# Retention then an expert layer: the third batch's transposes go to the crossbar, the fourth's first ones to another queue, eight stores are held back

## The chip, the cores and the metric

The kernel runs on one core of one Trainium2 chip. The metric is the device time of one execution in microseconds (us): before the change 311.78, the median of three runs (311.3 to 312.04).

## What is computed

Two stages, one after the other. The first is retention, attention without a softmax: for each of 8 batches and 8 heads, 576 positions of 64 values, the scores `q k^T / 8` are multiplied by a decay `gamma^(i - j)` for `j <= i` and by zero elsewhere, and then by `v`. The second takes the 4608 x 512 result as tokens through a layer with `g(h) = h * sigmoid(beta * h)`, 512 to 2048 and back to 512.

```python
def _attn_ref(q, k, v):
    B, H, S, D_ = q.shape
    scores = 1.0 / np.sqrt(D_) * np.matmul(q, k.transpose(0, 1, 3, 2))
    gamma = 1.0 - 2.0 ** (-5.0 - np.arange(H, dtype=np.float32))
    rel = np.arange(S)[:, None] - np.arange(S)[None, :]
    Dmat = np.where(rel >= 0, gamma[:, None, None] ** rel[None, :, :], 0.0)
    return np.matmul(scores * Dmat[None, :, :, :], v)

def _moe_ref(x, w_in, w_out, beta):
    h = x @ w_in
    return (h * (1.0 / (1.0 + np.exp(-beta * h)))) @ w_out
```

Inputs and output are float32; the kernel multiplies in bfloat16.

## The kernel before

**Tiles.** A batch's first 512 positions are 4 chunks of 128; its last 64 are joined with another batch's to a tail tile. `seq` lists all of them in order: indices 0 to 3 are batch 0's chunks, 4 to 7 batch 1's, 8 to 11 batch 2's, 12 to 15 batch 3's, 16 and 17 two tails, 18 to 21 batch 4's, and so on. The second stage works in blocks of 512 tokens, one a batch, and one block of tails.

**A batch's preparation.** `load_q` and `load_kv` bring queries, and keys and values chunk by chunk, through SyncE's DMA queue (lines 81 and 94). `pre_q` (L247) scales the queries to bfloat16, `pre` copies a chunk's keys (L273) and scales its values (L255); for batch 2 and later all of it is on GpSimd (POOL). Queries and keys have to be transposed as well. Up to batch 2 TensorE does it: `t_q` (L297, two per batch, 8 transposes of 128x128 each) and `t_k` (L303, one per chunk, 4 each) write to PSUM, and ScalarE (ACT) or VectorE (DVE) copies the result to `qT` or `kT` (L298, L304). From batch 3 on the DMA's crossbar does it: `x_q` and `x_k` issue a `dma_start_transpose` each for half a batch's queries or a pair of chunks, and `x_tail` for a tail, all through ACT's DMA queue (L281). `XB` is the first batch for which this holds.

**A batch's attention.** `first(i)` does a pair of chunks i and i + 1: the state update `a_st(i)` (L396, which needs no transposed tile, with ACT copies L401) and the scores `a_sc` of both (L323, from `kT` and `qT`; DVE masks them, L333). `outputs` multiplies the masked scores by the values (L366), adds the part of the state (L351), and copies to `xT` (L384), the second stage's input.

**The second stage.** `up` multiplies four 128-row pieces of `w_in` by `xT` (L413) and applies the activation on ACT (L415). `down` multiplies by `w_out` (L426); when the last of 2048 is added, DVE copies the result to `ot` (L433) and SyncE stores it (L436, 256 KB for a quarter of a block).

**The order is written out by hand.** `fill` is the list of all `up` and `down` calls. `merged` walks through it, and before item n it emits every other step with a due position of at most n. Each engine, and each DMA queue, runs its instructions in the order in which they were emitted; an instruction that waits for another engine or for a transfer holds up what comes behind it on its engine. Items 0 to 15 are block 0's `up`, from `d0` = 16 its `down`; from `u1` = 32 block 1's `up` (20 half items for two chunks each, then 6 whole ones), from 58 its `down`; `base[n]` is where block n starts: 74, 106, 138 for 2, 3, 4 (`base[1]` is 42). Where the steps around the change stand:

| step | due position before |
|---|---|
| `load_q(2)`, loads of chunks 8, 9 | 10.4 |
| loads of chunks 10 and 11 | 24.6, 26.1 |
| stores of block 0 | after 25, 26, 27, 31 |
| `pre_q(2, 0..3)`, on POOL | 41 to 44 |
| `pre(8)` to `pre(11)`, on POOL | 46.5 to 48 |
| `t_q(2, 0)`, `t_q(2, 1)` | 47.5, 48.5 |
| `t_k(8)`, `t_k(9)`; `first(8)` | 49.5, 50.5; 53 |
| `load_q(3)`; loads of chunks 12, 13 | 47; 49, 51 |
| `t_k(10)`, `t_k(11)`; `first(10)`; `outputs(8)` | 58.5, 59.5; 62; 67 |
| `pre_q(3, 0..3)`; `pre(12)`, `pre(13)` | 57 to 60; 61, 62 |
| `x_q(3, 0)`, `x_q(3, 1)`, `x_k(3, 0)`, on ACT's queue | 63, 64.5, 66.5 |
| stores of block 1 | after 61, 65, 69, 73 |
| loads of chunks 14, 15; `first(12)` | 64, 66; 77 |
| `load_tail(0)`, `x_k(3, 1)`, `load_tail(1)` | 78, 81.5, 88 |

Staging tiles for the output, `ot`, come from the four buffers (tag `wt`) through which the weights were loaded: blocks 0 to 3 have one each, block 4 takes block 0's again.

Of the kernel before, what the change touches and what calls it, by code (L numbers as in the profile page):

```python
# [19 lines left out]
def kernel(  # L20
# [10 lines left out]
    nc = tc.nc  # L31
# [9 lines left out]
    CB = MB // P  # L41
# [25 lines left out]

    NQ = 6
    E = CB
    XB = 3  # L70
    QB = 2
    q_tiles, kv_tiles = {}, {}

# [158 lines left out]
    batch, pair, live = {}, {}, {}  # L232
# [44 lines left out]
    def heads(t, p):  # L277
        return t[:, 2 * p:2 * p + 2, :].rearrange("p h d -> p (h d)")

    def turn(dst, src):  # L280
        nc.scalar.dma_start_transpose(dst.rearrange("p j pr s -> p (j pr) s"), src.rearrange("p j h d -> p (j h d)"))  # L281

    def x_q(b, u):
        turn(batch[b]["qT"][:, 2 * u:2 * u + 2], batch[b]["qs"][:, 2 * u:2 * u + 2])

    def x_k(b, u):
        kn, kT = pair[b, u]
        turn(kT, kn)

    def x_tail(i):  # L290
        turn(live[i]["qkT"], live[i]["qk"])
# [122 lines left out]
                             start=(ko == 0), stop=(ko == KO - 1))  # L414
        nc.scalar.activation(gts[m][:, fo, :, w], ph, ACT.Silu, scale=beta_sb[:, fo:fo + 1])  # L415

    pos_, ots = {}, {}

    def down(m, ms, f0, fn=4, n0=0, nn=d_model):

        gT = gts[m]
        if f0 == 0:
            pos_[ms] = psum.tile([P, d_model], F32, name="po", tag="mm", bufs=3)
        po = pos_[ms]
        for fo in range(f0, f0 + fn):
            nc.tensor.matmul(po[:, :nn], gT[:, fo, ms, :], w_out_sb[:, fo, n0:n0 + nn],  # L426
                             start=(fo == 0), stop=(fo == FO - 1))
        if f0 + fn < FO:
            return
        if ms == 0:  # L430
            ots[m] = stage.tile([P, MB // P, d_model], F32, name="ot", tag="wt", bufs=4)
        ot = ots[m][:, ms, n0:n0 + nn]
        nc.vector.tensor_copy(ot, po[:, :nn])  # L433
        if m < B:
            rows = out[m * S:m * S + MB].rearrange("(s i) n -> s i n", i=CB)
            nc.sync.dma_start(rows[:, ms, n0:n0 + nn], ot)  # L436
        else:
            for x in range(2):
                r0 = (2 * ms + x) * S + MB
                nc.sync.dma_start(out[r0:r0 + TL, n0:n0 + nn], ot[x * TL:(x + 1) * TL])  # L440
# [12 lines left out]
    def F(f, *a):  # L453
        return lambda: f(*a)
# [49 lines left out]
    fill = [F(up, 0, fo) for fo in range(FO)]  # L504
    d0 = len(fill)
    fill += [F(down, 0, ms, f0) for f0 in range(0, FO, 4) for ms in range(3)]
    fill += [F(down, 0, 3, f0) for f0 in range(0, FO, 4)]

    u1 = len(fill)
    fill += [F(up, 1, fo, 2 * x, 2) for x in range(2) for fo in range(10)]  # L510
    fill += [F(up, 1, fo) for fo in range(10, FO)]
    fill += [F(down, 1, ms, f0) for ms in range(MB // P) for f0 in range(0, FO, 4)]
    base = {1: u1 + 10}
    for n, m in enumerate(blocks[2:], 2):
# [6 lines left out]
    def second(i):  # L521
        for f in (a_O, lambda j: a_cross(j, False), a_x):
# [6 lines left out]
               [(d0 - 4 + 3.3 * g, F(cast_w_out, g)) for g in range(WG)],  # L529
               [(10.3, F(load_q, 1))] + [(10.3, F(load_kv, CB + n, (j,))) for n, j in keys_first],  # L530
               [(10.4, F(load_q, 2))] + [(10.4, F(load_kv, 2 * CB + n)) for n in range(2)],
               [(d0 + 8.6, F(load_kv, 2 * CB + 2)), (d0 + 10.1, F(load_kv, 2 * CB + 3))],
               [(d0 + 7, F(pre_q, 1, n)) for n in range(4)] + [(d0 + 10.6, F(t_q, 1, 0)), (d0 + 12.6, F(t_q, 1, 1))],
               [(d0 + 8, F(pre, 4, (0,))), (d0 + 8, F(pre, 5, (0,))), (d0 + 9, F(pre, 4, (1,))), (d0 + 9, F(pre, 5, (1,))),
                (d0 + 12.7, F(t_k, 4)), (d0 + 12.8, F(t_k, 5)), (d0 + 13.8, F(a_sc, 4)), (d0 + 13.81, F(a_sc, 5)),
                (d0 + 14.8, F(a_st, 4)), (d0 + 15.9, F(second, 4))],
# [16 lines left out]
    def pair_prep(i, at):  # L553
        b, c = seq[i]
        if b is None:
            return [(at - 31, F(load_tail, c)), (at - 21.5, F(pre, i)), (at - 21, F(load_tail, c + 1)),
                    (at - 13, F(pre, i + 1)), (at - 12, F(x_tail, i)), (at - 9.5, F(x_tail, i + 1))]
        n, st = full.index(i), []
        if b < XB:
            if c == 0:  # L560
                st += [(at - 12 + x, F(pre_q, b, x)) for x in range(4)]
                st += [(at - 5.5, F(t_q, b, 0)), (at - 4.5, F(t_q, b, 1))]
                st += [(at - 6.5 + x / 2, F(pre, i + x)) for x in range(CB)]
            return st + [(at - 3.5, F(t_k, i)), (at - 2.5, F(t_k, i + 1))]
        if c == 0:
            st += [(at - 30, F(load_q, b))] + [(at - 20 + x, F(pre_q, b, x)) for x in range(4)]
            st += [(at - 14 + 1.5 * x, F(x_q, b, x)) for x in range(2)]
        return st + [(at - 28, F(load_kv, n)), (at - 26, F(load_kv, n + 1)), (at - 16, F(pre, i)),
                     (at - 15, F(pre, i + 1)), (at - 10.5, F(x_k, b, c // 2))]

    todo = list(range(2 * CB, len(seq), 2))
    for n in range(1, B - 1):

        take = [i for i in todo if seq[i][0] == n + 1 or n == B - 2 or seq[i] == (None, 0) and n == CB - 1]
        todo = todo[len(take):]
        lo, hi = (base[n] + 11, base[n + 1] - 12) if n == 1 else (base[n] + 3, base[n + 1] - 8)
        at = [lo + x * (hi - lo) / (len(take) - 1) for x in range(len(take))]
        if len(take) == 2 and n > 1:
            at[1] -= 6
        for i, t in zip(take, at):  # L580
            st = pair_prep(i, t) + [(t, F(first, i))]
            if seq[i][0] is None:
                st.append((t + 5, F(second, i)))
            elif seq[i][1] == 0:
                st.append((t + 2, F(a_st, i + 1)))
            else:
                st.append((t + 5, F(outputs, i - 2)))
            streams.append(st)
# [32 lines left out]
```

## Time and profile before

| what | before |
|---|---|
| time, median of 3 runs | 311.78 us |
| time of the profiled execution | 311.92 us |
| span of the profiled execution, first to last instruction | 310.1 us |
| TensorE busy | 298.5 us |
| TensorE clock granted, mean | 0.998 |
| transposes by the crossbar, all on ACT's queue | 24 of 256 KB |
| TensorE transposes L297, L303 | 48 and 48 |
| one ACT copy of `qT`, of `kT` | 1012 ns, 586 ns |
| DMA moved | 52.79 MB |

In the profile PE is TensorE's matmul, PEld its weight load, SP SyncE, and a "q" behind an engine is its sequencer, which issues DMAs. A line of the chain or the timeline gives the start in us from the span's start, the duration, the engine, the line of the kernel, what is written and read, and how many instructions are merged in it; in brackets the idle time before it and what ended that. A line of DMA issues gives the transfer, the queue, how many, and the median time from issue to landing.

### The profile page before, as it was taken

To read this page: it belongs to the slowest core of one execution; us is meant where nothing else is said; L and a number is where in the kernel's file an instruction comes from. 1 tells how busy PE (TensorE), PEld (TensorE's weight loads), DVE (VectorE), ACT (ScalarE), POOL (GpSimd) and SP (SyncE) were. 2 spreads that over 40 slices of the span, in tenths; PEclk is the share of its full clock that TensorE was granted. 3 is DMA by queue.
4 is the path that set the end of the run, shared out by engine and by line. 5 is a ranking of instruction groups with operands and counts; after the bars stand their busy time and mean duration, and the time that the engine had idled before them with its cause. 6 is when DMAs were issued, how large, how long until landed. Compare 5 with 4: busy or idle time off the path is not lost.

```text
span 310.1 us, 5363 instructions
## 1 busy us (share of the span) xinstructions
PE 298.5 (96%) x2144; PEld 157.8 (51%) x2177; DVE 106.9 (34%) x191; ACT 143.0 (46%) x256; POOL 96.0 (31%) x131
## 2 busy tenths in 40 slices
PE   7789999999999999999999999999999999999995
PEld 5544456775544454454554545455545444444444
DVE  7554476342531342434430434043405420010012
ACT  5567626995138412560186117711673037207700
POOL 4663026846524282254308031902420000000000
PEclk9999999999999999999999999999999999999999
DMA  8999999998989999999897697968852110031011
GB/s 207 221 355 387 380 232 273 233 257 179 202 197 162 224 189 235 218 212 198 133 234 107 136 205 207 201 115 192 196 76 37 68 70 0 17 88 34 0 70 68
DMA packets 123897, 52.79 MB, mean 170 GB/s; under 512 B 105680, under 2 KB 116320, under 8 KB 123872
## 3 DMA queue, kind: packets, MB, share of 16 engines
q1 hardware_dynamic: 98496, 46.15, 61.5%
q10 hardware_dynamic: 25376, 6.30, 13.6%
q8 instruction: 17, 0.28, 0.4%
q14 instruction: 8, 0.07, 0.1%
HBM read 36.71 MB, written 9.44 MB: 149 GB/s over the span
## 4 chain that ended last, share of the span: by engine, by line
PE 85%; DMA 6%; SPq 5%; DVE 1%; issue 1%; ACT 1%; POOL 1%; POOLq 0%
PE po L426 40%; PE ph L413 35%; DMA wt<-in_moe_w_in_dram 4%; SPq L94 3%; PE O L366 3%; PE sc L323 3%; DMA qn<-in_q_dram 2%; PE O L351 2%; PE st L396 2%; SPq L178 1%; POOL qs L247 1%; PE T L297 1%; PE T L303 1%; ACT gT L415 0%; DVE xT L384 0%
## 5 line engine op out<-in xcount | busy, mean ns | idle before, releaser
L415 ACT ACTIVATE gT<-ph,beta_sb 128x512 bf16<-128x512 f32 (+1 forms) x154 | 99.2, 659 | 86.3 <-PE ph L413 83.4
L413 PE MATMUL ph<-xT,w_in_sb 128*128 128x512 bf16 (+1 forms) x600 | 129.3, 365 | 3.2 <-DVE w_in_sb L186 0.9
L426 PE MATMUL po<-w_out_sb,gT 128*128 128x512 bf16 (+2 forms) x591 | 126.7, 368 | 1.1 <-issue 0.3
L413 PEld LDWEIGHTS <-w_in_sb 128*128 128x128 bf16 x616 | 58.7, 98 | 65.0 <-DVE w_in_sb L186 2.3
L426 PEld LDWEIGHTS <-gT 128*128 128x128 bf16 x608 | 57.1, 98 | 62.5
L333 DVE TENSOR_TENSOR R<-sc,causal 128x512 bf16<-128x512 f32 x71 | 44.3, 684 | 68.9 <-PE sc L323 68.9
L433 DVE COPY ot<-po 128x512 f32<-128x512 f32 (+2 forms) x38 | 25.0, 662 | 92.1 <-PE po L426 92.0
L255 POOL TENSOR_TENSOR vn<-kvn,gv 128x512 bf16<-128x512 f32 x32 | 33.4, 1042 | 22.8 <-DMA kvn<-in_v_dram 11.5
L247 POOL TENSOR_TENSOR qs<-qn,gq 128x512 bf16<-128x512 f32 x24 | 24.3, 1042 | 33.2 <-DMA qn<-in_q_dram 33.2
L273 POOL CAST kn<-kvn 128x512 bf16<-128x512 f32 x32 | 19.6, 612 | 47.7 <-DMA kvn<-in_k_dram 47.3
L401 ACT CAST sbd<-st 64x256 bf16<-64x256 f32 x48 | 17.4, 362 | 15.0 <-PE st L396 14.3
L384 DVE CAST xT<-O 128x512 bf16<-128x512 f32 x24 | 15.8, 688 | 19.6 <-PE O L366 9.6
L384 ACT CAST xT<-O 128x512 bf16<-128x512 f32 x11 | 6.4, 586 | 32.2 <-PE O L351 25.2
L396 PE MATMUL st<-vn,kn 128*128 128x128 bf16 x128 | 12.4, 219 | 0.2 <-POOL vn L255 0.2
L396 PEld LDWEIGHTS <-kn 128*128 128x128 bf16 x128 | 9.3, 98 | 5.0 <-issue 0.2
L366 PE MATMUL O<-R,vn 128*64 128x128 bf16 x288 | 10.7, 221 | 0.0
L323 PE MATMUL sc<-qT,kT 64*128 64x128 bf16 x256 | 10.3, 217 | 0.4 <-ACT kT L304 0.2
L366 PEld LDWEIGHTS <-vn 128*64 128x64 bf16 x288 | 8.5, 110 | 4.1 <-issue 3.6
L323 PEld LDWEIGHTS <-kT 64*128 64x128 bf16 x288 | 8.1, 94 | 3.8 <-ACT kT L304 1.5
L304 ACT COPY kT<-T 128x512 bf16<-128x512 bf16 x12 | 6.9, 586 | 4.8 <-PE T L303 4.8
L208 PE MATMUL ph<-warm 128*128 128x128 f32 (+1 forms) x24 | 7.0, 429 | 1.2 <-DVE warm L119 1.2
L186 DVE CAST w_in_sb<-wt 128x256 bf16<-128x256 f32 (+1 forms) x14 | 6.0, 476 | 5.2 <-DMA wt<-in_moe_w_in_dram 5.2
(56 smaller groups left out, 90.2 us busy)
## 6 DMA issues: line engine op xcount, KB each, us to landing
qn<-in_q_dram SPq DMA_DIRECT2D x16, 512.0 KB, 5.8
kvn<-in_k_dram SPq DMA_DIRECT2D x32, 256.0 KB, 5.9
kvn<-in_v_dram SPq DMA_DIRECT2D x32, 256.0 KB, 5.6
out_dram<-ot SPq DMA_DIRECT2D x31, 256.0 KB, 2.7
wt<-in_moe_w_out_dram SPq DMA_DIRECT2D x4, 1024.0 KB, 9.5
wt<-in_moe_w_in_dram SPq DMA_DIRECT2D x4, 512.0 KB, 7.5
wt<-in_moe_w_in_dram SPq DMA_DIRECT2D x2, 1024.0 KB, 11.8
out_dram<-ot SPq DMA_DIRECT2D x9, 128.0 KB, 2.4
```

Source lines behind the costliest of these rows:

```text
L247: e.tensor_tensor(batch[b]["qs"][:, cs, hs], q_tiles[b][:, hs, cs].rearrange("p h i d -> p i h d"), gq[:, cs, hs].unsqueeze(3).to_broadcas ...
L255: nc.gpsimd.tensor_tensor(live[i]["vn"][:], kv_tiles.pop(i)[:, 1], gains(gv, c), ALU.mult)
L273: nc.gpsimd.tensor_copy(kn[:, c % 2], t[:, 0])
L323: nc.tensor.matmul(view(sc[j][:, p, :]), L["kT"][r, p, :], rhs, start=True, stop=True, skip_group_check=True)
L333: nc.vector.tensor_tensor(R[:, j], sc[j][:], causal4[:] if i == CB - 1 else m_b, ALU.mult)
L366: nc.tensor.matmul(O[j * D:(j + 1) * D, p, :], vn[:, 2 * p + j, :], R[:, j, p, :], start=p == 0 and not (early and crossed), stop=early or ...
L384: (nc.scalar.copy if on_act else nc.vector.tensor_copy)(x, O[:])
L396: nc.tensor.matmul(st[:, p, :], heads(L["kn"], p), heads(L["vn"], p), start=(c == 0 and p == 0), stop=True, skip_group_check=True)
L413: nc.tensor.matmul(ph, w_in_sb[:, ko, fo * P:(fo + 1) * P], xts[m][:, ko, :, w], start=(ko == 0), stop=(ko == KO - 1))
L415: nc.scalar.activation(gts[m][:, fo, :, w], ph, ACT.Silu, scale=beta_sb[:, fo:fo + 1])
L426: nc.tensor.matmul(po[:, :nn], gT[:, fo, ms, :], w_out_sb[:, fo, n0:n0 + nn], start=(fo == 0), stop=(fo == FO - 1))
L433: nc.vector.tensor_copy(ot, po[:, :nn])
```

## The change

Batch 2 is transposed by the crossbar instead of TensorE (`XB` from 3 to 2, so `t_q(2)` and `t_k(8..11)` are gone, and `x_q(2)`, `x_k(2)` come in). The crossbar transposes of queries for batches 2 and 3, and of their first pair of keys, are issued by SyncE; the others stay with ACT. The preparation of batch 2 is emitted earlier: `pre_q(2)` at 28.5, `x_q(2, 0)` and `x_q(2, 1)` at 28.6 and 28.7 and `x_k(2, 0)` at 29.6 (ahead of the load of chunk 11, now at 29.8), `pre(8)`, `pre(9)` at 29 and 30, `pre(10)`, `pre(11)` at 40 and 40.5, `x_k(2, 1)` at 58.5. `first(8)`, `first(10)` and `outputs(8)` move to 58, 64 and 69. The eight stores of blocks 0 and 1 are put on a list, and issued four at 69.5 and four at 82.

```diff
-    XB = 3
+    XB = 2
...
-    def turn(dst, src):
-        nc.scalar.dma_start_transpose(dst.rearrange("p j pr s -> p (j pr) s"), src.rearrange("p j h d -> p (j h d)"))
+    def turn(dst, src, on_sp=False):
+        (nc.sync if on_sp else nc.scalar).dma_start_transpose(dst.rearrange("p j pr s -> p (j pr) s"), src.rearrange("p j h d -> p (j h d)"))
 
     def x_q(b, u):
-        turn(batch[b]["qT"][:, 2 * u:2 * u + 2], batch[b]["qs"][:, 2 * u:2 * u + 2])
+        turn(batch[b]["qT"][:, 2 * u:2 * u + 2], batch[b]["qs"][:, 2 * u:2 * u + 2], b <= XB + 1)
 
     def x_k(b, u):
         kn, kT = pair[b, u]
-        turn(kT, kn)
+        turn(kT, kn, b <= XB + 1 and u == 0)
...
-    pos_, ots = {}, {}
+    pos_, ots, held = {}, {}, []
+
+    def release(n):
+        for _ in range(n):
+            nc.sync.dma_start(*held.pop(0))
...
-            nc.sync.dma_start(rows[:, ms, n0:n0 + nn], ot)
+            if m < 2:
+                held.append((rows[:, ms, n0:n0 + nn], ot))
+            else:
+                nc.sync.dma_start(rows[:, ms, n0:n0 + nn], ot)
...
-               [(d0 + 8.6, F(load_kv, 2 * CB + 2)), (d0 + 10.1, F(load_kv, 2 * CB + 3))],
-               [(d0 + 7, F(pre_q, 1, n)) for n in range(4)] + [(d0 + 10.6, F(t_q, 1, 0)), (d0 + 12.6, F(t_q, 1, 1))],
+               [(d0 + 8.6, F(load_kv, 2 * CB + 2)), (d0 + 12.6, F(x_q, XB, 0)), (d0 + 12.7, F(x_q, XB, 1)),
+                (d0 + 13.6, F(x_k, XB, 0)), (d0 + 13.8, F(load_kv, 2 * CB + 3)),
+                (base[2] - 4.5, F(release, 4)), (base[2] + 8, F(release, 4))],
+               [(d0 + 7, F(pre_q, 1, n)) for n in range(4)] + [(d0 + 12.5, F(pre_q, XB, n)) for n in range(4)] + [(d0 + 10.6, F(t_q, 1, 0)), (d0 + 12.6, F(t_q, 1, 1))],
...
-        if b < XB:
+        if b == XB:
             if c == 0:
-                st += [(at - 12 + x, F(pre_q, b, x)) for x in range(4)]
-                st += [(at - 5.5, F(t_q, b, 0)), (at - 4.5, F(t_q, b, 1))]
-                st += [(at - 6.5 + x / 2, F(pre, i + x)) for x in range(CB)]
-            return st + [(at - 3.5, F(t_k, i)), (at - 2.5, F(t_k, i + 1))]
+                return [(d0 + 13, F(pre, i + x, (0,))) for x in range(2)] + \
+                       [(d0 + 14, F(pre, i + x, (1,))) for x in range(2)]
+            return [(u1 + 8 + x / 2, F(pre, i + x)) for x in range(2)] + [(u1 + 26.5, F(x_k, b, 1))]
...
-        lo, hi = (base[n] + 11, base[n + 1] - 12) if n == 1 else (base[n] + 3, base[n + 1] - 8)
+        lo, hi = (base[n] + 16, base[n + 1] - 10) if n == 1 else (base[n] + 3, base[n + 1] - 8)
```

## The prediction

> **What bounds the kernel now.** First the page's busy line, the slices and the shares of the chain that ended last.
>
> ```profile
> PE 298.5 (96%) x2144; PEld 157.8 (51%) x2177; DVE 106.9 (34%) x191; ACT 143.0 (46%) x256; POOL 96.0 (31%) x131
> PE   7789999999999999999999999999999999999995
> DMA  8999999998989999999897697968852110031011
> PE 85%; DMA 6%; SPq 5%; DVE 1%; issue 1%; ACT 1%; POOL 1%; POOLq 0%
> ```
>
> TensorE is full from the fourth slice to the last but one, so a microsecond of TensorE work taken out shortens the span by one, and a microsecond of waiting put in lengthens it by one. The DMA engines are full too until about slice 22 (170 us): whatever is handed to them there comes late. Next I read the chain of waits from 57 to 92 us, where batch 2 is prepared.
>
> ```profile
> 62.24 0.45 PE T L297 x8
> 63.12 0.45 PE T L297 x8
> 64.00 0.22 PE T L303 x4
> 64.76 0.22 PE T L303 x4
> ...
> 71.70 0.65 PE po L426 x3
> 72.40 0.39 PE T L303 x4
> ...
> 73.65 0.22 PE T L303 x4
> ```
>
> The 32 transposes of batch 2 stand in the chain, eight in 0.45 us, and nothing idles beside them: they cost what they last. By the timeline fill item 58, the first `down` of block 1, begins at 71.54; a `down` item of four matmuls takes 0.865 us. (The 0.39 at 72.40 holds 0.17 that belongs to a matmul record missing before it.)
>
> **What is removed.** Two `t_q(2, u)` of 8 transposes and four `t_k` of 4: 32 x 0.0556 = 1.78 us of TensorE. With them go copies off the bound: on ACT one of 1.01 (L298) and four of 0.59 us (L304), on DVE one of 0.69. If nothing is late, the span falls by 1.78. Moving `first(8)` from 53 to 58, `first(10)` from 62 to 64 and `outputs(8)` from 67 to 69 changes no amount of TensorE work. ACT was busy 11.80 of the 13.0 us from 57 to 70, but there it loses 2.18 us of copies against TensorE's 1.33, so it does not become the pace.
>
> **What is added.** Four crossbar transposes of 256 KB. Their price comes from the queue rows.
>
> ```profile
> q1 hardware_dynamic: 98496, 46.15, 61.5%
> q10 hardware_dynamic: 25376, 6.30, 13.6%
> ```
>
> The 24 old transposes are all of q10: 13.6% of 310.1 over 24 is 1.76 us of all 16 engines each. On q1 a transfer of 0.262 MB costs 61.5% of 310.1 x 0.262/46.15 = 1.08 us. [...]
>
> **SyncE's queue** in the same stretch:
>
> ```profile
> 56.49 1.11 SPq L94 DMA_DIRECT2D kvn<-in_k_dram  x1
> ...
> 58.81 1.46 SPq L436 DMA_DIRECT2D out_dram<-ot  x2
> 60.36 0.42 SPq L94 DMA_DIRECT2D kvn<-in_k_dram  x1
> ...
> 61.83 2.72 SPq L436 DMA_DIRECT2D out_dram<-ot  x2
> 64.60 2.04 SPq L81 DMA_DIRECT2D qn<-in_q_dram  x2
> ```
>
> Keys and values of chunk 10, two stores of block 0, chunk 11, two stores, queries of batch 3. The stores leave (4 x 1.08 = 4.3 us of DMA), and `x_q(2,0)`, `x_q(2,1)`, `x_k(2,0)` come in after chunk 10 (3 x 1.76 = 5.3): the queries of batch 3 land some 1.0 us later. What SyncE now waits for is GpSimd's scaling of batch 2's queries:
>
> ```profile
> 55.17 4.04 POOL L247 TENSOR_TENSOR qs<-qn,gq 128x512 bf16<-128x512 f32 x4 [2.40 <-DMA qn<-in_q_dram]
> 65.45 0.61 POOL L273 CAST kn<-kvn 128x512 bf16<-128x512 f32 x1 [1.57 <-DMA kvn<-in_k_dram]
> 72.84 4.04 POOL L247 TENSOR_TENSOR qs<-qn,gq 128x512 bf16<-128x512 f32 x4 [4.37 <-DMA qn<-in_q_dram]
> ```
>
> It starts when the queries land and keeps that time: its first half is ready at 57.2, all of it at 59.2, the keys of chunks 8 and 9 two casts of 0.61 later (60.4). SyncE reaches `x_q(2,0)` at 58.7, so the waits there are under 0.5 us each; queued behind them are chunk 11 and the queries of batch 3. In order of service, from the values of chunk 10 (landed about 62.3, when GpSimd takes them up at 62.83): the three transposes land at 64.1, 65.8, 67.6, the keys of chunk 11 at 68.6, and GpSimd has cast them at 69.4 (before: 66.1). The queries of batch 3 land near 73.7 (before 72.8).
>
> **Where TensorE meets them.** `first(8)`, item 58: 71.54 less 24 transposes (1.33) and less `first(8)` (0.22 + 0.55) and the state update (0.22) that move behind it is 69.2; after `a_st(8)` the scores want `qT` and `kT` at 69.4. They have been there since 67.6: cost nothing, with 1.8 us of cover; if the transposes took 3 us each it would be a stall of 2. `first(10)`, item 64: 69.2 + 0.77 + 0.22 + six items of 0.865 + `a_st(10)` 0.22 = 75.6. Its keys come by `x_k(2,1)`, which ACT issues behind the state copies of `a_st(8)`, at about 69.6, just after chunk 11 is cast (69.4). Queued behind it on ACT are only the copies of `a_st(9)`, wanted at item 69, 5 us on. How long such a transpose takes from issue to landing I bound by its own kind, each taken from the page of its window (windows 112 to 118, 144 to 146, 162 to 163, 123 to 124):
>
> ```profile
> kT<-kn ACTq DMA_TRANSPOSE x2, 3.6
> kT<-kn ACTq DMA_TRANSPOSE x1, 6.8
> kT<-kn ACTq DMA_TRANSPOSE x1, 6.0
> kT<-kn ACTq DMA_TRANSPOSE x1, 10.1
> ```
>
> 3.6 is with little beside it; 6.8 and 6.0 beside key and value loads; 10.1 beside a whole query load. At 69.6 the queue holds the end of batch 3's queries and then keys and values, nearest to the middle rows: I take 6.5, landing at 76.1, a stall of 0.5. The ends are 3.6 (none) and 10.1 (79.7, a stall of 4.1).
>
> **Batch 3's part.** Three of its transposes leave ACT's queue for SyncE's. Before, ACT stood at them from 76.0 to 83.5 while TensorE ran on `down` items that need no ACT, so nothing is gained there now. On SyncE they wait for GpSimd: queries from 73.7 to 77.7, then two chunks of 1.55 us; `x_k(3,0)` goes out near 81.5 and lands near 86. `first(12)` wants it at 91.45 + 0.22 - 1.3 = 90.4: 4 us of cover, and the same as before if that is gone (it landed 9.7 us after 80.0 then). Behind the waiting ones on SyncE are chunks 14 and 15 and the tail loads. In the old order they stood behind stores of block 1 that waited for their copies (the last until 89.6); these are held now, so they come no later. The old kernel has no transposes on two queues, so what one costs the other has no row: at least nothing, at most a wait for the other's landing. The latter holds `x_q(3,0)` until 76.1, 1 to 2 us, inside the cover of 4, and `x_k(2,1)` until 67.6, before it is reached: I take nothing. [...]
>
> **The held stores** (8 of 1.08 us of DMA) go out from item 70 on and after 82; their buffers are wanted again by block 4. Behind them on SyncE stand the tail loads, whose transposes fall at item 97. Cover over 10 us; gone, it would be a wait of some us at item 109.
>
> **Sum.** -1.78 + 0 + 0.5 = -1.3 us on the profiled execution: span 310.1 to 308.8. It took 311.92 with 1.8 around its span; the median of the runs is 311.78, which becomes 310.5. A change below 0.2% (0.62 us) can't be told from none here.
>
> **Rivals.** (1) No stall: `x_k(2,1)` lands within 6.0 us of its issue. For it: the ACT row of 162 us and the transposes of 3.6. Against: the saturated queue. -1.78, so 310.0. (2) The stall eats the gain: landing 7.2 to 8.4 us after issue, because the queries of batch 3 are still moving at 72 to 74 or chunk 11 is cast a microsecond late (65.45 now waits on its DMA). Stall 1.2 to 2.4, time 311.2 to 312.4, middle 311.7. (3) Slower, at the same place: `x_k(2,1)` shares the engines with batch 3's queries throughout, as the row of 10.1 did; then `first(10)` stalls 4.1 and the time is 311.8 - 1.8 + 4.1 = 314.1. It decides from a landing 8.4 us after issue (a stall of 1.78 + 0.62). For it: queries 1.0 us later than before, and all DMA slices at 9. Against: most of them are served by 72. (4) The change does not do what it says, ACT pacing the half items and the removed 1.33 us coming back as idle TensorE: the time then falls only by the 0.44 of the last two `t_k`, to 311.3. ACT's greater loss of work speaks against it; I put it into (2).
>
> **How the numbers follow.** The forecast, a stall of about 0.5 (0.1 to 1.1), gets 0.37; rival 1 0.25; rivals 2 and 4 0.16; rival 3 0.22. Faster by over 0.2% is the forecast and rival 1: 0.62. The likeliest is 310.5, with a range of its own of 310.1 to 311.1. For 8 in 10 the range goes from 309.5 (no stall, and the one wait of 0.60 us that TensorE has at 165 gone in part) up to 313.0, which leaves out the far part of rival 3.
>
> **What would show it.** 32 fewer L297 and L303 matmuls; 28 transposes in all, 6 of them on SyncE; item 58 near 69.2; waits of TensorE at L323 for `kT` by DMA near 69 (none) and 75.6 (0.5). Wrong would be: a wait over 1.8 us there, a wait at `first(8)`, or a new wait of TensorE after 90 us.

## The result: 3.6% slower

| what | before | after |
|---|---|---|
| time, median | 311.82 us | 322.35 us (4 runs, 320.87 to 325.56) |
| ratio to before, 95% interval | | 1.0361 [1.031, 1.0413] |
| span of the profiled execution | 310.1 us | 323.7 us |
| TensorE busy; mean granted clock | 298.5 us; 0.998 | 299.2 us; 0.979 |
| L297 and L303 transposes | 48 and 48 | 32 and 32 |
| crossbar transposes, on SyncE's queue | 24, 0 | 28, 6 |

The prediction was 310.5 with a range up to 313.0, so it was wrong, and on the other side. First the page of the changed kernel: the busy line, three rows of slices (8.1 us each), and the shares of the chain that ended last. (Lines have moved by four: `down` is now L430; the held stores go out from L421.)

```profile
PE 299.2 (92%) x2112; PEld 156.6 (48%) x2145; DVE 106.1 (33%) x190; ACT 140.1 (43%) x251; POOL 96.5 (30%) x131
PE   7799999993299989999999999999999999999995
PEclk9999999998579999999999999999999999999999
DMA  8999999999995996999869396989883110032011
PE 66%; DMA 15%; SPq 12%; POOL 4%; issue 2%; DVE 1%; POOLq 0%; ACTq 0%
```

There is one hole in TensorE's row, in slices 10 and 11 (73 to 89 us), and the granted clock drops right under it and one slice beyond. 32 matmuls are gone, yet TensorE's busy time has grown: some of the rest ran slower. TensorE's share of the chain fell from 85% to 66%; transfers went from 6% to 15%, and SyncE's queue from 5% to 12%. The next view is the timeline of TensorE there (start, duration, engine, line, written and read tiles, count; in brackets the idle time before it and what ended it).

```profile
69.01 0.39 PE L396 MATMUL st<-vn,kn 128*128 128x128 bf16 x4
69.33 0.62 PE L323 MATMUL sc<-qT,kT 64*128 64x128 bf16 x16
...
71.84 3.62 PE L430 MATMUL po<-w_out_sb,gT 128*128 128x512 bf16 x16
86.86 0.58 PE L396 MATMUL st<-vn,kn 128*128 128x128 bf16 x4 [11.40 <-ACT sbd L401]
87.71 1.03 PE L323 MATMUL sc<-qT,kT 64*128 64x128 bf16 x16 [0.27 <-DMA kT<-kn]
88.68 4.02 PE L430 MATMUL po<-w_out_sb,gT 128*128 128x512 bf16 x9
92.92 2.34 PE L430 MATMUL po<-w_out_sb,gT 128*128 128x512 bf16 x10 [0.22 <-issue]
...
119.67 0.62 PE L323 MATMUL sc<-qT,kT 64*128 64x128 bf16 x16 [1.21 <-DMA kT<-kn]
```

Up to item 64 everything is as worked out: `first(8)` begins at 69.01 (69.2 was expected), its scores wait for nothing. Then `a_st(10)`, ready to run at about 75.5, stands for 11.40 us, and not for a transpose but for ACT's state copies of `a_st(9)`. ACT's timeline says why they came so late (ACTq is its sequencer, which issues the transposes):

```profile
69.80 0.74 ACT L401 CAST sbd<-st 64x256 bf16<-64x256 f32 x2
84.53 1.33 ACTq L281 DMA_TRANSPOSE kT<-kn  x1
85.96 0.76 ACT L401 CAST sbd<-st 64x256 bf16<-64x256 f32 x2 [15.42 <-issue]
```

ACT runs nothing for 15.42 us. "issue" is time in which the profile shows no wait. What stands at its head is the one transpose that ACT issues here, `x_k(2, 1)`: reached at 70.5, gone out at 84.53. Its keys had landed at 69.18, and GpSimd had cast them to bfloat16 by 69.84:

```profile
69.23 0.61 POOL L273 CAST kn<-kvn 128x512 bf16<-128x512 f32 x1 [4.87 <-DMA kvn<-in_k_dram]
```

SyncE's queue has what did end at that moment; below it stand the same transfer and the one that followed it, in the chain that ended last:

```profile
79.53 2.40 SPq L281 DMA_TRANSPOSE qT<-qs  x1
```

```profile
79.53 4.83 DMA qT<-qs
...
84.53 3.14 DMA kT<-kn
```

This is `x_q(3, 1)`. It took 4.83 us from issue to landing: it landed at 84.35, and 0.18 us later `x_k(2, 1)` went out. Nothing in the kernel's source connects the two. The waits that the finished program carries do (DMAHW0 to DMAHW7 are the eight semaphores that this program's transfers count up when they have landed; first ACT's `x_k(2, 1)`, then SyncE's `x_q(3, 0)` and `x_q(3, 1)`, each of which waits for the earlier transfer on its own semaphore):

```
89 L281 DmaTransposeAnt kT_864<-kn_863 128x8x128 [waits DMAHW2_49,DMAHW5_49,DMAHW1_49,DMAHW7_49,DMAHW0_49,Pool_49]
...
48 L281 DmaTransposeAnt qT_1016<-qs_1015 128x8x128 [waits DVE_49,PE_49,DMAHW2_49,Activation_49,Pool_49]
51 L281 DmaTransposeAnt qT_1016<-qs_1015 128x8x128 [waits DMAHW5_49,Pool_49]
```

Semaphores 7, 0 and 1 belong to batch 2's three transposes on SyncE (0 also to a load of chunk 13's keys, landed at 78.03), 2 and 5 to batch 3's two. So `x_k(2, 1)` waits for the landing of transposes that are emitted four and a half and six items after it; the second of them landed 0.18 us before it went out. The software layer that turned the emitted calls into this program recorded them in an order of its own across the queues, and put into `x_k(2, 1)` a wait for each of the five transposes of the other queue that are recorded ahead of it.

The last view is that of the stretches around the hole (stretch, length, busy time and count of PE, PEld, DVE, ACT and POOL, granted clock, DMA share, GB/s).

```profile
75.30:79.30 4.00, 0.16 (x1) 0.00 (x0) 0.00 (x0) 0.00 (x0) 4.00 (x5) 1.00 0.96 192
79.30:86.90 7.60, 0.04 (x1) 0.07 (x2) 0.00 (x0) 0.73 (x2) 3.27 (x5) 0.50 1.17 205
86.90:92.90 6.00, 5.53 (x29) 2.55 (x31) 3.07 (x5) 0.73 (x2) 0.00 (x0) 0.50 0.74 196
92.90:100.00 7.10, 7.03 (x71) 4.08 (x72) 2.77 (x5) 1.32 (x3) 4.25 (x6) 1.00 0.87 224
```

At 79.3, after 3.8 us of idling (from 75.5), the granted clock falls from 1.00 to 0.50, and it stays so for 6.0 us after the wait is over: nine `down` matmuls take 4.02 us from 88.68, and ten take 2.34 us from 92.92. TensorE worked for 5.53 of the 6.0 us at half the clock, and half of that, an estimated 2.8 us, was lost. The sum: 11.40 + 0.27 (the scores behind it) + 1.21 (a wait for `kT` at 118) + 2.8, less 1.78 for the transposes and 0.60 for a wait that the kernel before had and this one has not, is 13.3; the spans differ by 13.6. That wait is this line of TensorE's timeline before:

```profile
165.24 2.10 PE L413 MATMUL ph<-xT,w_in_sb 128*128 128x512 bf16 x9 [0.60 <-ACT gT L415]
```

### The profile page after: what moved, and what is told of

It is laid out like the page before. It is cut to its first block, busy times and chain, and to the rows that moved or that the text cites. A ratio compares the mean times of both kernels' runs of the same rounds, so it can differ in the third digit from the quotient of the medians.

```text
span 323.7 us, 5302 instructions
## 1 busy us (share of the span) xinstructions
PE 299.2 (92%) x2112; PEld 156.6 (48%) x2145; DVE 106.1 (33%) x190; ACT 140.1 (43%) x251; POOL 96.5 (30%) x131
## 4 chain that ended last, share of the span: by engine, by line
PE 66%; DMA 15%; SPq 12%; POOL 4%; issue 2%; DVE 1%; POOLq 0%; ACTq 0%
PE po L430 33%; PE ph L413 26%; SPq L94 8%; DMA kT<-kn 4%; DMA qn<-in_q_dram 4%; DMA wt<-in_moe_w_in_dram 4%; POOL qs L247 2%; PE O L366 2%; PE sc L323 2%; SPq L81 2%; DMA qT<-qs 1%; PE O L351 1%; DMA tln<-in_k_dram 1%; PE st L396 1%; SPq L178 1%
## 5 line engine op out<-in xcount | busy, mean ns | idle before, releaser
L430 PE MATMUL po<-w_out_sb,gT 128*128 128x512 bf16 (+2 forms) x591 | 128.4, 371 | 1.2 <-issue 0.5
L430 PEld LDWEIGHTS <-gT 128*128 128x128 bf16 x608 | 57.6, 99 | 64.3 <-issue 2.9
L437 DVE COPY ot<-po 128x512 f32<-128x512 f32 (+2 forms) x38 | 25.0, 661 | 86.0 <-PE po L430 85.9
L401 ACT CAST sbd<-st 64x256 bf16<-64x256 f32 x48 | 17.4, 363 | 29.6 <-issue 15.4
L396 PE MATMUL st<-vn,kn 128*128 128x128 bf16 x128 | 12.6, 222 | 11.7 <-ACT sbd L401 11.4
L396 PEld LDWEIGHTS <-kn 128*128 128x128 bf16 x128 | 9.3, 99 | 16.6 <-issue 12.0
L323 PE MATMUL sc<-qT,kT 64*128 64x128 bf16 x256 | 10.7, 223 | 1.9 <-DMA kT<-kn 1.5
L323 PEld LDWEIGHTS <-kT 64*128 64x128 bf16 x288 | 8.4, 96 | 5.5 <-DMA kT<-kn 1.9
L262 POOL TENSOR_TENSOR kn<-tln,gq 128x512 bf16<-128x512 f32 x4 | 4.2, 1042 | 13.4 <-DMA tln<-in_q_dram 10.0
```

The source lines that it names most:

```text
L323: nc.tensor.matmul(view(sc[j][:, p, :]), L["kT"][r, p, :], rhs, start=True, stop=True, skip_group_check=True)
L396: nc.tensor.matmul(st[:, p, :], heads(L["kn"], p), heads(L["vn"], p), start=(c == 0 and p == 0), stop=True, skip_group_check=True)
```

## Experiments

Diffs are against the changed kernel, where nothing else is said. Two causes were to be told apart at first: transposes of two queues being kept apart, and the held stores or busy engines making the transfers late.

**Batch 3's transposes back to ACT**, so that SyncE has only batch 2's.

```diff
-        turn(batch[b]["qT"]..., batch[b]["qs"]..., b <= XB + 1)
+        turn(batch[b]["qT"]..., batch[b]["qs"]..., b <= XB)
...
-        turn(kT, kn, b <= XB + 1 and u == 0)
+        turn(kT, kn, b <= XB and u == 0)
```

> Batch 3's three first transposes go back to ACT's queue; batch 2's stay as in the change. Theory (cross-queue wait): in the changed kernel x_k(2,1) on ACT was issued at 84.53, just after SyncE's x_q(3,1) landed at 84.35, and the state copies behind it held TensorE for 11.4 us; here no SyncE transpose of batch 3 exists, so x_k(2,1) goes out near 70 and the time is 310.0 to 311.5. Rival (the transpose is late because the DMA engines are full): the same transfers are in the way, so the wait stays near 10 us and the time near 320.

Measured 318.83 us, ratio 1.0231 [1.0206, 1.0256]: a miss for the theory, and nearer to the rival's time. The waits shrank to 4.33 and 2.70 us but were not gone. TensorE's, ACT's and SyncE's timelines:

```profile
79.39 0.38 PE L396 MATMUL st<-vn,kn 128*128 128x128 bf16 x4 [4.33 <-ACT sbd L401]
82.47 1.03 PE L323 MATMUL sc<-qT,kT 64*128 64x128 bf16 x16 [2.70 <-DMA kT<-kn]
```

```profile
77.04 1.35 ACTq L281 DMA_TRANSPOSE kT<-kn  x1
```

```profile
71.81 1.06 SPq L94 DMA_DIRECT2D kvn<-in_v_dram  x1
```

With no later transpose on SyncE, `x_k(2, 1)` still went out at 77.04 and not at 70. The load in the last line is the values of chunk 13; it took 5.1 us and landed at 76.89, just before. The program's wait list for `x_k(2, 1)` now has only batch 2's semaphores, 7, 0 and 1, and 1 was counted up once more by that load. (The profile puts ACT's idle time down to GpSimd, which ended an instruction at the same time; from GpSimd the wait list has only the cast of chunk 11's keys, done at 68.6.) So there is a second tie: in these programs all transfers of both queues take the eight semaphores in turn, and a transfer waits for the landing of the one eight places before it in the recorded order, whatever that one carries (here from 76.89 to 77.04, 0.15 us after it).

**`x_k(2, 1)` on SyncE's queue too.**

```diff
-        turn(kT, kn, b <= XB + 1 and u == 0)
+        turn(kT, kn, b <= XB + 1 and u == 0 or b == XB)
```

> All of the change, but x_k(2,1) is issued by SyncE too, so that no ACT transpose stands between SyncE's. Theory: ACT is never held; x_k(2,1) goes out behind chunk 13 on SyncE at about 75.5 and lands near 79.5, TensorE waits some 4 us at the scores of chunk 10 instead of 11.4, time 312.5 to 315. Rival (full DMA engines): landing and wait about as in the change, near 320.

Measured 315.2 us (312.71 to 316.22), ratio 1.0101 [1.0054, 1.0149], just above the range. Of batches 2 and 3, ACT now issues only `x_k(3, 1)`, late; `x_k(2, 1)` goes out at 74.01, behind the loads on its queue, and lands at 78.76.

```profile
78.81 1.04 PE L323 MATMUL sc<-qT,kT 64*128 64x128 bf16 x16 [3.13 <-DMA kT<-kn]
```

TensorE waits 3.13 us. In the profiled execution the clock was halved from 77.9 to 84.7, which cost an estimated 2.95 us more (half of the 5.89 us that TensorE was busy in it). The spread of 3.5 us goes with the clock: the four runs, from the fastest, had a mean of 1.0, 0.995, 0.989 and 0.987.

**The stores not held.**

```diff
-            if m < 2:
-                held.append((rows[:, ms, n0:n0 + nn], ot))
-            else:
-                nc.sync.dma_start(rows[:, ms, n0:n0 + nn], ot)
+            nc.sync.dma_start(rows[:, ms, n0:n0 + nn], ot)
...
-                (base[2] - 4.5, F(release, 4)), (base[2] + 8, F(release, 4))],
```

> All of the change but the held stores: blocks 0 and 1 are stored at once again. Theory: the wait of x_k(2,1) for batch 3's queries on SyncE stays, and SyncE comes later for four stores: 321 to 326. Rival (the release of the stores in front of the tail loads, or their burst, causes the loss): 310 to 312.

Measured 314.5 us, ratio 1.0085 [1.0063, 1.0106]: 7.9 us less than the changed kernel, a miss for the theory of that moment, and above the rival's 310 to 312. On ACT and on TensorE:

```profile
71.62 1.33 ACTq L281 DMA_TRANSPOSE kT<-kn  x1
```

```profile
78.98 1.03 PE L323 MATMUL sc<-qT,kT 64*128 64x128 bf16 x16 [3.42 <-DMA kT<-kn]
```

Batch 3's transposes are on SyncE's queue as in the changed kernel, but `x_k(2, 1)` no longer waits for them. The program's wait list has batch 2's semaphores and one more: it is recorded right behind the loads of chunk 13 here, ahead of batch 3's transposes, and its own semaphore is that of the transfer eight places before it, chunk 11's values (landed 71.52, gone out at 71.62). In the changed kernel's program, with the stores out of the way, six more of SyncE's transfers are recorded ahead of it.

**The held stores alone**, in the kernel before (diff against it: `held`, `release` and the two release steps as in the change).

> The kernel before with the eight stores held and nothing else changed. Theory: SyncE is not late for anything there, 311.2 to 312.4. Rival (the held stores cost by themselves): over 314.

Measured 312.1 us over 10 runs, ratio 1.0014 [0.9996, 1.0033]. Holding cost nothing that can be measured here, where all transposes by the crossbar are on ACT's queue.

**Chunk 11 loaded early again**, at its old 26.1, to see if the keys' readiness plays a part.

```diff
-               [(d0 + 8.6, F(load_kv, 2 * CB + 2)), (d0 + 12.6, F(x_q, XB, 0)), (d0 + 12.7, F(x_q, XB, 1)),
-                (d0 + 13.6, F(x_k, XB, 0)), (d0 + 13.8, F(load_kv, 2 * CB + 3)),
+               [(d0 + 8.6, F(load_kv, 2 * CB + 2)), (d0 + 10.1, F(load_kv, 2 * CB + 3)), (d0 + 12.6, F(x_q, XB, 0)), (d0 + 12.7, F(x_q, XB, 1)),
+                (d0 + 13.6, F(x_k, XB, 0)),
```

> The change with one thing moved: the load of chunk 11 stands at its old position 26.1, ahead of SyncE's transposes, so that the keys of chunk 11 are cast near 65 instead of 69. Theory (x_k(2,1) waits for the landing of SyncE's x_q(3,1)): nothing is gained, x_k(2,1) goes out near 84 and the time stays at 319 to 326. Rival (the data of x_k(2,1) is late): it goes out near 70, time 310 to 312.

Measured 322.23 us (2 runs), ratio 1.0328 [1.0298, 1.0359]. On GpSimd and on ACT:

```profile
64.13 0.61 POOL L273 CAST kn<-kvn 128x512 bf16<-128x512 f32 x1 [0.41 <-DMA kvn<-in_k_dram]
```

```profile
83.02 1.33 ACTq L281 DMA_TRANSPOSE kT<-kn  x1
```

The keys are cast 18 us before the transpose goes out; it goes out 0.10 us after `x_q(3, 1)` landed (82.92). The wait is for the other queue's transposes and not for the keys.

**Batch 3's on ACT and the stores not held**, the first and the third edit together.

> As e1 (batch 3's transposes on ACT's queue), and the stores of blocks 0 and 1 not held. Theory (the program lets eight transfers be in flight over both queues together, each waiting for the landing of the eighth before it in recorded order; holding the stores lets SyncE's loads of chunks 14 and 15 be recorded ahead of x_k(2,1)): here x_k(2,1) follows the values of chunk 11, near 71.5, not 77.0 as in e1; TensorE waits about 3 to 4 us instead of 7.0; time 313 to 315. Rival (e1's wait was the full DMA engines): a wait of 7 us or more, 318 or above.

Measured 314.18 us, ratio 1.0081 [1.0055, 1.0107], as expected. `x_k(2, 1)` goes out at 71.71, after chunk 11's values (landed 71.62), and TensorE waits 2.91 us:

```profile
78.46 1.03 PE L323 MATMUL sc<-qT,kT 64*128 64x128 bf16 x16 [2.91 <-DMA kT<-kn]
```

Between the first experiment and this one only the hold differs, and it moves the transpose from 77.04 to 71.71: the hold makes the recorded order late, by the one tie or by the other.

**Everything for batch 2 early, on SyncE:** chunk 11 at 26.1 as in the fifth experiment, `x_k(2, 1)` at 41 on SyncE's queue.

```diff
-        turn(kT, kn, b <= XB + 1 and u == 0)
+        turn(kT, kn, b <= XB + 1 and u == 0 or b == XB)
...
-            return [...] + [(u1 + 26.5, F(x_k, b, 1))]
+            return [...] + [(u1 + 9, F(x_k, b, 1))]
```

> The change with the load of chunk 11 at 26.1 and x_k(2,1) on SyncE at 41, right behind x_k(2,0), so that every SyncE transpose comes ahead of every ACT one and x_k(2,1) is ahead of batch 3's loads. Theory: it lands near 70, before the scores of chunk 10 ask for it at 75.6; no wait of TensorE over 0.5 us between 60 and 95, no half clock, time 309.5 to 310.8, under the kernel before. Rival (the crossbar transposes cost TensorE time wherever they stand, because batch 3's loads come later for them): a wait at the scores of chunk 8 or 12, 312 or above.

Measured 313.97 us over 12 runs, ratio 1.0058 [1.0039, 1.0077]; a miss. `x_k(2, 1)` lands at 70.25 and TensorE has no wait from 60 to 95, so the rival's wait at the scores is not there either. But `x_k(3, 1)` is still on ACT's queue, beside batch 3's other three on SyncE's. ACT and TensorE:

```profile
97.53 1.80 ACTq L281 DMA_TRANSPOSE kT<-kn  x1
```

```profile
100.12 2.10 PE L413 MATMUL ph<-xT,w_in_sb 128*128 128x512 bf16 x9 [2.33 <-ACT gT L415]
```

It goes out 0.17 us after a store of SyncE's landed (97.36; issued 93.38), and behind it stood an activation of block 2's `up`, for which TensorE waited 2.33 us. The store stands eight places before it in the recorded order: the tie of the first experiment, one batch later.

**The same with all four of batch 3's on ACT.**

```diff
-..., b <= XB + 1)
+..., b <= XB)
...
-        turn(kT, kn, b <= XB + 1 and u == 0)
+        turn(kT, kn, b <= XB)
```

(and the two early steps as above)

> As e7, but batch 3's three first transposes on ACT's queue as in the kernel before. Theory: their waits fall where ACT has only copies to do, nothing on TensorE, 309.5 to 311.3. Rival (ACT held by them delays the state copies): a wait of TensorE at a state update of batch 2, 312 or above.

Measured 317.32 us over 5 runs, ratio 1.0184 [1.0156, 1.0211]. A miss, and much as the rival had it:

```profile
85.23 1.33 ACTq L281 DMA_TRANSPOSE qT<-qs  x1
```

```profile
87.47 0.61 PE L351 MATMUL O<-qT,sbd 128*128 128x128 bf16 x4 [4.67 <-ACT sbd L401]
```

`x_q(3, 0)` stands on ACT until 85.23, when the transfer eight places before it, the values of chunk 15, has landed (85.14), and state copies behind it; TensorE waits 4.67 us at L351, and the clock is halved from 85.9 to 92.7.

**All of batches 2 and 3 on SyncE**, ACT's first crossbar transposes being the tails'.

```diff
-        turn(kT, kn, b <= XB + 1 and u == 0)
+        turn(kT, kn, b <= XB + 1)
```

(and the two early steps as above)

> As e7, and x_k(3,1) on SyncE too, so that ACT issues no crossbar transpose before the tails'. Theory: in e7 x_k(3,1) stood on ACT until 97.53, when the store recorded eight transfers before it had landed (97.36), and TensorE waited 2.3 us for the activations behind it; that wait goes, the one of 1.1 us near 127 stays, and the time falls by 2.3 to 311.2 to 312.0. Rival (ACT was held by its DMA issue as such): the wait moves to another place, 313 to 314.5.

Measured 309.73 us over 12 runs, ratio 0.9943 [0.9923, 0.9963]: better than expected, and faster than the kernel before. TensorE's waits are 0.20 us at `first(8)` and 1.07 near 125, where ACT stands at the transpose of batch 4's first keys until 124.9; the clock is not halved (1.00 from 60 to 300). ACT and TensorE:

```profile
121.48 3.43 ACTq L281 DMA_TRANSPOSE kT<-kn  x1
```

```profile
125.70 1.89 PE L413 MATMUL ph<-xT,w_in_sb 128*128 128x512 bf16 x8 [1.07 <-ACT gT L415]
```

-1.78 - 0.60 + 0.20 + 1.07 = -1.1, and the span went from 310.1 to 308.9. This last wait is not the tie: what the transpose waits for by its list was done by 116.4 (GpSimd's cast at 115.4, and a store eight places before it that landed at 116.35). Its issue itself took 3.43 us, where the one before it on ACT (119.75) took 1.25; why is not shown.

**The same, batch 4's first `x_k` 2.5 items later** (diff against the version before).

```diff
-                     (at - 15, F(pre, i + 1)), (at - 10.5, F(x_k, b, c // 2))]
+                     (at - 15, F(pre, i + 1)), (at - (8 if b == XB + 2 and c == 0 else 10.5), F(x_k, b, c // 2))]
```

> As e9, and batch 4's first x_k is issued 2.5 items later on ACT, so that GpSimd's cast is done when ACT comes to it (in e7 it stood there from 124.0 to 127.4 and TensorE waited 1.1 us). Theory: that wait goes or shrinks below 0.5 us, time 310.2 to 311.2, 0.2% or more under the kernel before. Rival (the transpose then lands too late for the scores of chunk 18): a wait at the scores near 135, 312 or above.

Measured 309.52 us over 6 runs, ratio 0.9924 [0.9897, 0.995]. The wait at 125 is gone, and the issue at 124.92 takes 1.25 us; GpSimd's cast, which the expectation named as the cause, had been done in time in the version before too. In this execution the page's slices have no hole left, and the only wait for a transpose is the one of the last line (sum, count, largest).

```profile
PE   7789999999999999999999999999999999999995
PEclk9999999999999999999999999999999999999999
PE sc L323 <- DMA kT<-kn: 0.6, 1, 0.6
```

The last line stands at `first(8)`, 0.62 us. -1.78 - 0.60 + 0.62 = -1.8, the difference of the spans (308.3 to 310.1). Against the last version this one is not told apart; both beat the kernel before.

## Why the prediction was wrong

*What is removed:* right. 32 transposes fewer; in the last two experiments the spans come out within 0.1 us of sums that have the 1.78 in full, so no other engine took over the pace, and rival 4 is out.

*SyncE's queue and the landings:* right. The three transposes were to land at 64.1, 65.8 and 67.6, and landed at 64.70, 66.95 and 67.87; the keys of chunk 11 at 68.6 (69.18); the queries of batch 3 at 73.7 (74.65). The price of a transpose taken from the queue's row held roughly: the three had landed 4.7 us after the values of chunk 10 (63.16), where three times 1.76 is 5.3. `first(8)` met no wait.

*The step that failed* is the sentence on transposes on two queues: "at least nothing, at most a wait for the other's landing ... `x_k(2,1)` until 67.6, before it is reached: I take nothing". A wait for the other's landing it was, but I counted only the transposes emitted earlier. The program made it wait for later ones also: `x_q(3, 0)` and `x_q(3, 1)` are emitted after it and recorded ahead of it, and it stood on ACT from 70.5 until the second of them had landed at 84.35, and went out at 84.53. That only transposes ahead of it in the source could hold it was an assumption of mine, taken from no run.

*What stands behind it* was named rightly, the copies of `a_st(9)`, but they were called "wanted at item 69, 5 us on". That was the wrong consumer: `a_st(10)` at item 64 waited for them too (11.40 us, released by `sbd`). So a late transpose on ACT hit TensorE through ACT's queue before it did through `kT`.

*The landing:* 6.5 us taken, with bounds of 3.6 and 10.1. It took 6.7 and 7.3 where it went out at 71.7 (without the hold), 3.1 at 84.53. Its size was right; its start was not. Rival 3 had the right place and the wrong mechanism, contention of transfers, and about a third of the wait. What was named as a sign of being wrong, a wait over 1.8 us near 75.6, is there, one step earlier than named (L396 and not L323); the new wait after 90 us is there too, at 118.

*Batch 3's part:* the tie works in the other direction too. `x_k(3, 0)`, expected to go out near 81.5, did so at 87.80, when `x_k(2, 1)` had landed (87.67); everything behind had moved by then, and no wait of TensorE is left of it. `x_k(3, 1)`, issued by ACT at 109.72 and landed at 119.62, is the 1.21 us at 118: 9.9 us, at the upper one of my bounds.

*The held stores:* alone they cost nothing that was measured (312.1 us, ratio 1.0014), as I said. What I didn't see is that stores that stand at their place also keep SyncE's later transfers behind `x_k(2, 1)` in the recorded order. That is worth 322.35 - 314.5 = 7.9 us here.

*The clock* had no term at all: an estimated 2.8 us of the 13.6.

Open: why the layer records `x_k(2, 1)`, emitted at 58.5, behind steps emitted at 63 to 66 when the stores are held. The runs show that it does and that the hold decides it; the rule by which it orders is not known from them. The issue of 3.43 us in the last but one experiment is open as well.

## What to carry to other kernels

Put all transposes of a stretch on one DMA queue, as the two versions did that beat the kernel before (309.73 and 309.52 us), and change the queue only where all of the old one have landed: here a transpose on the second queue waited, from 70.5 to 84.53 us, for ones that stand after it in the source, and everything on its engine waited with it (ACT idle for 15.42 us). Before an edit that moves DMA starts between engines, read the waits of the finished program for the moved instruction, and count transfers of both queues eight back: there stood the transfers whose landings, at 76.89, 97.36 and 85.14, a transpose waited for in three of these runs. Price a long wait of TensorE with the slow clock that comes with it: the waits of 2.91 us and more in the table below had one, for 3.4 us or longer.

## What the runs showed of the hardware

In seven of these eight kernels the granted clock fell to 0.50 during or just after a wait of TensorE, and stayed there for some 3.4, 6.8 or 13.6 us (one profiled execution each):

| kernel | wait of TensorE | halved from, to | length |
|---|---|---|---|
| changed | 11.40 | 79.3 to 92.9 | 13.6 |
| chunk 11 early | 9.61 | 77.9 to 91.5 | 13.6 |
| batch 3's on ACT | 4.33 and 2.70 | 79.7 to 86.6 | 6.9 |
| `x_k(2, 1)` on SyncE | 3.13 | 77.9 to 84.7 | 6.8 |
| early, batch 3's on ACT | 4.67 | 85.9 to 92.7 | 6.8 |
| stores not held | 3.42 | 78.7 to 82.1 | 3.4 |
| batch 3's on ACT, stores not held | 2.91 | 78.3 to 81.7 | 3.4 |
| early, on SyncE | 2.33 | not halved | |

The stretch of the kernel without held stores, in the columns of the earlier windows, shows what it costs:

```profile
78.70:82.10 3.40, 3.12 (x22) 1.55 (x23) 2.48 (x4) 0.00 (x0) 3.40 (x4) 0.50 1.34 236
```

TensorE worked for 3.12 us of it, and half of that, an estimated 1.6 us, was lost: a wait of 3.4 cost 5.0. The lengths are, within 0.1 us, once, twice and four times 3.4. The shortest wait with a halved clock is 2.91 us, and the one of 2.33 us had none; what decides it, and what sets the length, these executions do not show.
